# One emission order for another in a three-part kernel: first stage, last step and tail rewritten, some weight preparation on other engines

## The chip, the cores and the metric

The kernel runs on one core of one Trainium2 chip. The metric is device time in microseconds (us) of one execution; lower is better. Three executions of the kernel before gave 519.78, 521.58 and 523.94 us, a median of 521.58. The engines of a core run their own instruction queues in order: PE (TensorE, matmul), DVE (VectorE), ACT (ScalarE), POOL (GpSimd) and SP (SyncE), which here issues nearly all DMAs. They wait for each other by semaphores.

## What is computed

A gated linear attention, a two-layer network with a leaky ReLU, and a soft mixture of experts, in float32:

```python
for t in range(S):                       # attention, per batch and head; S = 768, D = 48
    state = alpha[t, :, None] * state + k[t][:, None] * v[t][None, :]
    y[t] = q[t] @ state
x = y as [3072, 384]
h = x @ w_in                             # [3072, 2048]
g = maximum(h, 0) + alpha_ff * minimum(h, 0)
x2 = g @ w_out                           # [3072, 384]
logits = x2 @ phi                        # 32 slots
slot_input = softmax(logits, over tokens).T @ x2
slot_out[e] = maximum(slot_input[e] @ w1[e], 0) @ w2[e]     # 8 experts, 4 slots each
out = softmax(logits, over slots) @ slot_out
```

## The kernel before

The 3072 tokens are cut into eight steps (i = 0 to 7) of 384 tokens, each of three chunks of 128. One step goes through these parts:

- **Preparation** (`pre_first` for step 0, `pre_gen` for the others): the decays `al` are clamped (L212), multiplied up from the left by three scans (L219, into `P`) and from the right by three more (L229, in place in `al`); then `q` is multiplied by `P` (L222, on POOL) and `k` by the result of the second scans (L234, on DVE for step 1, on POOL later). ACT checks the range of `al` in two passes (`flag`, L173).
- **Attention** (`att_chunk`), per chunk: `k` transposed on PE (L257, `kt`) and copied by ACT (L259); scores `sc` (L251), masked by DVE into `tmp` (L266); the state's increment `kv` (L277), added and scaled on DVE into the next state `S` (L285, L286), which ACT copies into a matmul layout (L290, L291); the output `y` (L297). `split_x` makes a rounded high part `xh` (ACT, L537) and the remainder `xl` (DVE, L538).
- **First layer** (`h_part`, one of 16 per step): nine logical matmuls of 128x384 with the high and low parts of x and w_in (L358), a scaled copy `tn` on ACT (L367) and a maximum on DVE (L368, `g`).
- **Second layer and logits** (`g_part`): after every fourth `g`, a matmul `lg` with the product of w_out and phi (L401). `g` is also turned for the slot sums: on PE in steps 0 and 7 (L381, `tr`), in the other steps by DVE blockwise (L386, `st`) and 32 DMAs on SP (L394, `gT`).
- **Softmax over tokens and slot sums** (`soft_gen`): logits summed by a matmul `L` (L427), exponentials, small transposes on DVE (L452), the slot sums `u` (L410 from `gT`, L416 in steps 0 and 7), accumulated by L470 or L472.
- **Weights** (`conv_gen`): w_in and w_out come as eight pairs of 768 KB of int64 bits (float64) and are turned into float32 in the kernel. The 16 pieces have letters: A, C, E, G, I, K, M, O are w_in 0 to 7; B, D, F, H, J, L, N, P are w_out 0 to 7. For each: a load (L104); the high word scaled (L111 on ACT, or L109 on DVE for the letters in `P_DVE`) and the low word scaled (L112, ACT); two integer operations on DVE (L123, L124); an addition on POOL (L125). A w_in piece is then rounded to `wi` on ACT (L128), and the remainder is taken from it (L129), on POOL for letters in `POOL_OPS`, else on DVE. A pair of w_out pieces is written to DRAM (L140), transposed on PE (L146, `wT`, three groups of four), copied by ACT into `X` (L147), and multiplied by phi (L153, `wps`).
- **Tail** (`tail_steps`): slot inputs, expert layers (L593, L614), a gather (L622, L627) and the outputs (L639, copies L642 and L644, DMAs L647). Weights w1 and w2 are loaded by `feed` (L514) and `feed_wide` (L504) in the last steps, in the order of need.

Nothing is scheduled by a tool: each part is a Python generator that emits a few instructions at a time, and four strings of letters say which generator emits next. The order of the letters is the order of the instructions on every engine's queue:

```python
    for c in START + STEADY * (NSTEP - 3) + LAST:
        next(s[c])
    k.tail()
```

`l` loads al, k, q of a step (step 0: with v, a third at a time), `w` loads v, `p` is one piece of preparation, `x`, `y`, `z` are one piece of attention of chunk 0, 1, 2, `h` one first-layer part, `g` one second-layer part, `s` one piece of softmax, `d` two small loads, `f` and `m` weight loads for the tail, `c` and `C` one step's softmax over slots (L490 to L496); capital A to P are one piece of that letter's weight preparation. START runs once, with 8 of the 128 `h`; STEADY runs five times; LAST and TAIL end the kernel.

`RAW_SLOT` names the pieces whose raw load takes a slot of its own in the pool of 22; the others share two wide buffers, two pieces to a buffer. Since a letter string sets all queues at once, moving a letter moves its DMAs on SP as well as its work on DVE, ACT, POOL and PE. A DMA waits for the eighth DMA before it and for its buffer.

Of the kernel before, what the change touches and what calls it, by code (L numbers as in the profile page):

```python
# [29 lines left out]
class Kern:  # L30
# [60 lines left out]
    def conv_gen(self, kind, n):  # L91
        nc = self.nc
        add = nc.gpsimd if CONV_NAMES[CONV.index((kind, n))] in POOL_OPS else nc.vector
        name = CONV_NAMES[CONV.index((kind, n))]
        if name in RAW_SLOT:
            raw = self.slot(f"raw{name}")
# [10 lines left out]
        yield  # L107
        if name in P_DVE:
            nc.vector.tensor_scalar_mul(out=p, in0=p, scalar1=2.0 ** -112)  # L109
# [95 lines left out]
    def pre_gen(self, i):  # L205
# [22 lines left out]
        for c, r in enumerate(parts):  # L228
# [4 lines left out]
            yield  # L233
        (nc.vector if i == 1 and "k" not in POOL_OPS else nc.gpsimd).tensor_tensor(out=k, in0=k, in1=G, op=ALU.mult)  # L234
        d["ready"] = 3
# [322 lines left out]
    def tail_steps(self):  # L558
# [72 lines left out]
        def output(ch, i):  # L631
# [13 lines left out]
            rows = self.a["out"][2 * i * T:2 * (i + 1) * T, CH * ch:CH * (ch + 1)]  # L645
            queue = nc.gpsimd if "stuvwxyz"[4 * ch + i] in TAIL[-LAST_OUT:] else nc.sync
            queue.dma_start(out=rows.rearrange("(t p) c -> p t c", p=128), in_=ot)  # L647
# [10 lines left out]
    def tail(self):  # L658
        steps = self.tail_steps()
        for c in TAIL:  # L660
            steps[c]()
# [2 lines left out]

CH = T // 2
PE_TURN = (0, NSTEP - 1)
POOL_OPS = "CDEHLNQRTVX"
LAST_OUT = 1
RAW_SLOT = "BCDEGHJLMO"
P_DVE = "KNOP"  # L670
PRE_POOL = ()
START = "lpldlpAFABxppFpxyBpCBpxyAlCxAHpyxEOFwDpMByGzwHAJCpEzCGDIppppyzzDhpEDGpphhHEIEpDxIFgxzGFDJNIJCPJBHLhGhJHxhHKLKLggyyKBhLMggMLOxKgKOlIMLPFNxyNJpNpPypppphzNzpPPPNyOpOMppg"
STEADY = "lhgzzhghghhzgxxpghghghghgpspphhxgyyspsghspxhxhgsggpghshzzywgpyypp"
LAST = "hhhhzgggghhgzghhhghggsgxxxshhghxsygyshygmxszgyzghhgghhz1zQhhfhyhggQzgghshghgfgfcghghsghfshghmQgQzhgffhcshhgghfgfggghfccfcffhfhgsghsfhgcfsgfgss2sffssfsf"
TAIL = "FabCcFFdgFCehFifkjFomFFqvlstunprzyxw"
W_ORDER = ([("w1", 4 * q + e, hf) for q in range(2) for hf in range(2) for e in range(4)]
           + [("w2", e, ch) for ch in range(2) for e in range(8)])

# [11 lines left out]
def streams(k):  # L690
    def loads():
        for c in range(3):
            k.att_load(0, ("al", "k", "q", "v"), c)
            yield
        for i in range(1, NSTEP):
            k.att_load(i, ("al", "k", "q"))
            yield

    def v_loads():
        for i in range(1, NSTEP):  # L700
            k.att_load(i, ("v",))
            yield

    def pres():
        yield from k.pre_first()
        for i in range(1, NSTEP):
            yield from k.pre_gen(i)

    def atts(c):
        for i in range(NSTEP):  # L710
            yield from k.att_chunk(i, c)

    def small():
# [33 lines left out]
def general_path(tc, nslots, ys, **a):  # L747
# [41 lines left out]
    with ExitStack() as ctx:  # L789
# [81 lines left out]
```

## Time and profile before

| | |
|---|---|
| median of three executions | 521.58 us (519.78 to 523.94) |
| profiled execution, its own time | 523.21 us |
| its span, first to last instruction | 521.1 us |
| outside the span | 2.1 us |
| mean granted TensorE clock | 0.93 of full |
| PE / DVE / ACT / POOL busy | 87% / 66% / 41% / 16% of the span |

The views are of one profiled execution. Times in them are us from the first instruction. PE's rows come in "x" counts of hardware matmuls, two to a logical one. The granted clock is a share of TensorE's full speed. A bracket at the end of a timeline row gives the idle time of the engine before it and what ended it.

### The profile page before, as it was taken

The page shows a single profiled execution, that of the slowest core. Times are in us where ns is not written, and L with a number is a line of the kernel's source. Part 1 is how long each engine was busy: PE and PEld are TensorE (multiplying, and loading weights), DVE is VectorE, ACT ScalarE, POOL GpSimd, SP SyncE. Part 2 cuts the span into 40 slices and gives each one's busy share as a digit, 9 for nine tenths or more (in the row PEclk, how much of TensorE's full clock was granted, in tenths as well). Part 3 has the DMA queues.
Part 4 walks back from the last instruction along what each step waited for, and adds up shares of the span by engine and source line. Part 5 has one row for each costly group of instructions (what it writes and reads, how often), then busy time and mean ns, then how long its engine had stood idle before and what let it go on. Part 6 is the DMA issues. An engine that isn't in the chain of part 4 may idle for free.

```text
span 521.1 us, 11082 instructions
## 1 busy us (share of the span) xinstructions
PE 454.3 (87%) x4524; PEld 371.3 (71%) x4524; DVE 345.2 (66%) x684; ACT 214.5 (41%) x408; POOL 82.2 (16%) x47
## 2 busy tenths in 40 slices
PE   2663489899999999999999999999997999959881
PEld 1452479788988887888688788788875888643561
DVE  6867963699379879869877986995673543451222
ACT  0783425763562543354244335423422345332122
POOL 1135351344002202200220220021000001000000
PEclk9985757778999999999999999999999999989986
DMA  8994440614006345645643554512664948979856
GB/s 282 406 415 188 181 182 1 232 42 178 36 2 241 79 83 115 238 100 122 243 99 69 153 207 85 122 62 59 127 182 86 332 107 313 403 306 413 355 172 199
DMA packets 41595, 93.99 MB, mean 180 GB/s; under 512 B 5056, under 2 KB 29120, under 8 KB 41536
## 3 DMA queue, kind: packets, MB, share of 16 engines
q1 hardware_dynamic: 41392, 92.61, 54.3%
q8 instruction: 37, 0.61, 0.5%
q0 software_dynamic: 144, 0.59, 0.3%
q14 instruction: 22, 0.18, 0.1%
HBM read 66.45 MB, written 7.86 MB: 143 GB/s over the span
## 4 chain that ended last, share of the span: by engine, by line
PE 70%; DVE 10%; ACT 6%; SPq 4%; DMA 4%; issue 3%; POOL 1%; ACTq 0%; POOLq 0%
PE h L358 36%; PE y L297 5%; PE lg L401 4%; PE sc L251 4%; SPq L394 4%; PE u L410 3%; PE o L614 2%; PE h L593 2%; PE wps L153 2%; PE tr L381 2%; PE kv L277 2%; DMA rawB<-w_out 2%; DVE P L219 2%; PE kt L257 2%; DVE al L229 2%
## 5 line engine op out<-in xcount | busy, mean ns | idle before, releaser
L358 PE MATMUL h<-xh,wi 128*128 128x384 f32 x768 | 221.7, 356 | 9.2 <-ACT xh L537 8.8
L358 PEld LDWEIGHTS h<-xh,wi 128*128 128x128 f32 x768 | 145.1, 194 | 28.3 <-issue 16.5
L358 PE MATMUL h<-xl,wi 128*128 128x384 f32 x384 | 132.6, 345 | 0.0
L367 ACT ACTIVATE tn<-h,alp 128x384 f32<-128x384 f32 x128 | 73.8, 583 | 128.6 <-PE h L358 123.5
L368 DVE TENSOR_TENSOR g<-h,tn 128x384 f32<-128x384 f32 x128 | 69.2, 549 | 83.7 <-ACT tn L367 75.1
L358 PEld LDWEIGHTS h<-xl,wi 128*128 128x128 f32 x384 | 74.8, 195 | 1.2 <-DVE xl L538 0.3
L386 DVE STREAM_TRANSPOSE st<-g 128x384 f32<-128x384 f32 x96 | 53.1, 564 | 0.5 <-DMA gT<-st 0.3
L222 POOL TENSOR_TENSOR q<-q,P 128x1536 f32<-128x1536 f32 x7 | 24.4, 3481 | 149.7 <-DVE Z L221 114.8
L251 PE MATMUL sc<-q,k 48*128 48x128 f32 x384 | 33.2, 313 | 2.3 <-DVE tmp L266 2.3
L297 PE MATMUL y<-tmp,v 128*32 128x128 f32 x768 | 30.4, 299 | 3.8 <-DVE xl L538 2.5
L251 PEld LDWEIGHTS sc<-q,k 48*128 48x128 f32 x384 | 27.3, 209 | 8.3 <-issue 5.0
L257 PE MATMUL kt<-cst,k 128*128 128x128 f32 x80 | 14.9, 317 | 19.7 <-DVE k L197 10.7
L266 DVE TENSOR_TENSOR tmp<-sc,cst 128x512 f32<-128x512 f32 x48 | 30.5, 675 | 1.8 <-PE sc L251 1.4
L401 PE MATMUL lg<-g,wpr 128*32 128x384 f32 x256 | 30.8, 496 | 0.8 <-DVE g L368 0.8
L297 PEld LDWEIGHTS y<-tmp,v 128*32 128x32 f32 x768 | 22.9, 119 | 9.7 <-issue 4.0
L219 DVE TENSOR_TENSOR_SCAN P<-al,Z 128x512 f32<-128x512 f32 x21 | 26.8, 1293 | 0.2
L229 DVE TENSOR_TENSOR_SCAN al<-al,Z 128x512 f32<-128x512 f32 x21 | 26.4, 1264 | 0.2
L257 PEld LDWEIGHTS kt<-cst,k 128*128 128x128 f32 x80 | 10.6, 161 | 22.0 <-DVE k L197 10.9
L234 POOL TENSOR_TENSOR k<-k,al 128x1536 f32<-128x1536 f32 x6 | 17.4, 2905 | 51.8 <-DVE al L229 51.8
L290 ACT COPY S<-S 64x256 f32<-64x256 f32 x20 | 8.1, 406 | 41.8 <-DVE S L286 37.0
L410 PE MATMUL u<-gT,dT 128*32 128x512 f32 x144 | 20.9, 596 | 1.4 <-DMA gT<-st 1.4
L490 POOL COPY cr<-c 128x384 f32<-128x384 f32 x8 | 4.0, 507 | 110.5 <-DVE st L386 57.9
(211 smaller groups left out, 594.5 us busy)
## 6 DMA issues: line engine op xcount, KB each, us to landing
w<-w SPq DMA_DIRECT2D x28, 768.0 KB, 8.6
gT<-st SPq DMA_DIRECT2D x192, 96.0 KB, 2.2
al<-alT SPq DMA_DIRECT2D x7, 768.0 KB, 5.6
k<-kT SPq DMA_DIRECT2D x7, 768.0 KB, 7.1
q<-qT SPq DMA_DIRECT2D x7, 768.0 KB, 8.5
v<-vT SPq DMA_DIRECT2D x7, 768.0 KB, 4.2
out<-ot SPq DMA_DIRECT2D x7, 576.0 KB, 4.9
w_out_f<-wo SPq DMA_DIRECT2D x4, 768.0 KB, 4.0
```

What stands on the lines that cost most here:

```text
L219: nc.vector.tensor_tensor_scan(P[:, r], al[:, r], Z[:, r], 0.0, ALU.mult, ALU.add)
L229: nc.vector.tensor_tensor_scan(G[:, r][:, ::-1], G[:, r][:, ::-1], Z[:, r][:, ::-1], 0.0, ALU.mult, ALU.add)
L251: nc.tensor.matmul(sc[h][:, p], K[r, p, c], Q[r, p, c], start=True, stop=True)
L257: nc.tensor.transpose(kt[:, p * 128:(p + 1) * 128], K[:, p, c], self.ident)
L266: nc.vector.tensor_tensor(out=m, in0=sc[h], in1=self.tri[:, None, :].to_broadcast([128, NP, 128]), op=ALU.mult)
L297: nc.tensor.matmul(y[32 * g:32 * g + 32, kt], lhsT, rhs, start=start, stop=stop, skip_group_check=True)
L358: nc.tensor.matmul(h, w[ft // 2][:, kt, fs], x[:, kt], start=(n == 0), stop=(n == 8))
L367: nc.scalar.activation(out=t, in_=h, func=AF.Copy, scale=al)
L368: nc.vector.tensor_tensor(out=g, in0=h, in1=t, op=ALU.max)
L386: nc.vector.transpose(out=self.stage.rearrange("p t b f j -> p (t b) f j")[:, :, f], in_=g.rearrange("p (n j) -> p n j", j=32))
L401: nc.tensor.matmul(self.lg[32 * jj:32 * jj + 32], self.wpr[:, 4 * fb + jj], self.g[4 * fb + jj], start=(fb == 0), stop=(fb == 3))
L410: nc.tensor.matmul(u[32 * q:32 * q + 32], dT[:, t], self.gT[q][:, t], start=(t == 0), stop=(t == 2))
```

## The change

Four tables and the letter strings differ; no function does. w_in pieces A and K take their remainders (L129) on POOL instead of DVE. The high words of C and L are now scaled on DVE (L109) and those of K and N on ACT; O and P stay on DVE. G and L give up slots of their own and N gets one, so that G shares a wide buffer with I. START has the same letters in a new order. STEADY, LAST and TAIL hold the same letters too, some of them moved by a few places.

```diff
-POOL_OPS = "CDEHLNQRTVX"
+POOL_OPS = "ACDEHKLNQRTVX"
 LAST_OUT = 1
-RAW_SLOT = "BCDEGHJLMO"
-P_DVE = "KNOP"
+RAW_SLOT = "BCDEHJMNO"
+P_DVE = "CLOP"
 PRE_POOL = ()
-START = "lpldlpAFABxppFpxyBpCBpxyAlCxAHpyxEOFwDpMByGzwHAJCpEzCGDIppppyzzDhpEDGpphhHEIEpDxIFgxzGFDJNIJCPJBHLhGhJHxhHKLKLggyyKBhLMggMLOxKgKOlIMLPFNxyNJpNpPypppphzNzpPPPNyOpOMppg"
-STEADY = "lhgzzhghghhzgxxpghghghghgpspphhxgyyspsghspxhxhgsggpghshzzywgpyypp"
...
+START = "llplpBAAFxBdppFpxpyDCpBxAClxAAypyHpFEGByCwxMzJzpHODIEpGCBPzpDpwpzhpEpGpKIhIpHJFDDEyDghxFFIhGElNJhCJJLHHxhHLGxzyLKygKBMhggLLOMKgxxKgPMLONIyppzNJNPypNhpzOPMpppPpPyNpgpO"
+STEADY = "hlzgzzhghghhpghxxpgghghghgppsxghyyspgshhspxhghgssxpghhzzypygwpypg"
...
-TAIL = "FabCcFFdgFCehFifkjFomFFqvlstunprzyxw"
+TAIL = "FFabCcFdgeFCFhifkFjoFmlFqvstunprzyxw"
```

DVE's queue, at the end of step 0's attention. Names are tile and number; `al1` and `P1` are step 1's decays and products, `St` and `S` the state after chunk 2 of step 0, `xl0` the remainder of step 0's last chunk, which the first `h` needs. Before:

```order
L212 TENSOR_SCALAR al1_241<-al1_241 128x1536
L214 COPY Z_95<-al1_241 128x12
L215 MEMSET al1_241 128x13
L219 SCALAR_TENSOR_TENSOR P1_302<-al1_241,Z_95 128x512 x3
L221 MEMSET Z_95 128x12
L285 TENSOR_TENSOR St_397<-kv_387,S_284 128x256
L286 TENSOR_TENSOR S_396<-St_397,pe_121 128x256
L538 TENSOR_TENSOR xl0_267<-y_402,xh0_266 128x3x128
```

With the change:

```order
L215 MEMSET al1_239 128x13
L285 TENSOR_TENSOR St_391<-kv_381,S_284 128x256
L286 TENSOR_TENSOR S_390<-St_391,pe_125 128x256
L219 SCALAR_TENSOR_TENSOR P1_292<-al1_239,Z_95 128x512
L123 SCALAR_TENSOR_TENSOR rawD_211<-rawD_211 128x768
L124 TENSOR_SCALAR rawD_211<-rawD_211 128x768
L219 SCALAR_TENSOR_TENSOR P1_292<-al1_239,Z_95 128x512 x2
L221 MEMSET Z_95 128x12
L538 TENSOR_TENSOR xl0_263<-y_406,xh0_262 128x3x128
```

The two state operations moved ahead of the three scans, and the two integer operations of piece D moved from behind `xl0` to between the scans.

PE's queue, between the first `h` parts (`wi0`, `wi1` are w_in 0 and 1) and step 1's first attention work (`kt` from `k1`). Before, the end of the third `h` and what follows:

```order
L358 MATMUL h_487<-xh0_266,wi1_358 128x384
L146 MATMUL wT_509<-cst_91,wo0_213 128x128 x4
L257 MATMUL kt_518<-cst_91,k1_243 128x128 x4
L251 MATMUL sc0_515<-q1_245,k1_243 128x128
L251 MATMUL sc1_516<-q1_245,k1_243 128x128
L251 MATMUL sc0_515<-q1_245,k1_243 128x128
L251 MATMUL sc1_516<-q1_245,k1_243 128x128
L381 MATMUL tr_533<-cst_91,g_446 128x128 x3
```

With the change, the end of the second `h` and what follows:

```order
L358 MATMUL h_469<-xh0_262,wi0_233 128x384
L146 MATMUL wT_495<-cst_91,wo0_216 128x128 x4
L146 MATMUL wT_501<-cst_91,wo0_216 128x128 x4
L146 MATMUL wT_509<-cst_91,wo0_216 128x128 x4
L153 MATMUL wps_515<-phi_94,X0_494 128x32 x12
L381 MATMUL tr_530<-cst_91,g_447 128x128 x3
L358 MATMUL h_535<-xh0_262,wi1_333 128x384
```

`kt` of step 1 stands right behind that third `h`. The third group of `wT`, the 12 `wps` and one `tr` moved from behind `kt` to ahead of it; before, four more `sc` stood between them.

POOL's queue, from the second weight piece to step 1's `q`. Before:

```order
L125 TENSOR_TENSOR rawA_144<-rawA_144 128x768
L125 TENSOR_TENSOR wo1_294<-rawA_144 128x768
L125 TENSOR_TENSOR rawC_211<-rawC_211 128x768
L129 TENSOR_TENSOR wi1_358<-rawC_211,wi1_358 128x768
L222 TENSOR_TENSOR q1_245<-q1_245,P1_302 128x1536
L125 TENSOR_TENSOR wo0_213<-rawD_300 128x768
```

With the change:

```order
L125 TENSOR_TENSOR rawA_144<-rawA_144 128x768
L129 TENSOR_TENSOR wi0_233<-rawA_144,wi0_233 128x768
L125 TENSOR_TENSOR wo1_294<-rawA_144 128x768
L125 TENSOR_TENSOR rawC_213<-rawC_213 128x768
L129 TENSOR_TENSOR wi1_333<-rawC_213,wi1_333 128x768
L125 TENSOR_TENSOR wo0_216<-rawD_211 128x768
L222 TENSOR_TENSOR q1_243<-q1_243,P1_292 128x1536
```

The remainder of piece A was added behind its sum, and the sum of piece D moved ahead of step 1's `q`.

Elsewhere in words. SP issues all loads of step 0 first and then B, A, F (before: A, F, B, behind two small loads). In STEADY one `h` moved ahead of `kt`, `L` stands one `h` earlier, and the `lg` that followed `u` now stands ahead of it. In LAST, groups of `ct` (L493) that stood three in a row are set apart by other matmuls. In TAIL the second and third expert outputs `o` (L614) stand together, and the first output matmuls (L639) that stood between them follow.

## Rows read from the trace of the kernel before

**Rows 1.** Page, part 1: busy us (share of span), instructions.
```profile
PE 454.3 (87%) x4524; PEld 371.3 (71%) x4524; DVE 345.2 (66%) x684; ACT 214.5 (41%) x408; POOL 82.2 (16%) x47
```

**Rows 2.** Windows: length, busy us of PE, PEld, DVE, ACT, POOL, granted clock, DMA.
```profile
39.00:52.00 13.00, 4.16 (x31) 3.35 (x23) 10.43 (x9) 5.25 (x8) 7.28 (x3) 0.50 0.47 191
52.00:65.00 13.00, 5.91 (x28) 5.49 (x26) 11.70 (x15) 5.29 (x8) 4.90 (x3) 0.76 0.49 181
65.00:78.00 13.00, 11.00 (x56) 9.80 (x56) 8.30 (x7) 2.98 (x6) 6.89 (x3) 0.50 0.49 183
117.00:130.00 13.00, 12.23 (x123) 10.96 (x123) 12.67 (x17) 4.73 (x10) 5.11 (x2) 0.87 0.46 178
...
199.00:243.00 44.00, 44.00 (x470) 36.70 (x461) 35.84 (x77) 18.49 (x39) 6.41 (x2) 1.00 0.55 148
```

**Rows 3.** Waits of PE, whole span: waiting line, releaser, us, times, longest.
```profile
PE kt L257 <- DVE k L234: 9.1, 1, 9.1
PE h L358 <- ACT xh L537: 8.8, 1, 8.8
...
PE o L639 <- DVE ss L627: 2.6, 2, 1.3
...
PE u L410 <- DMA gT<-st: 1.4, 2, 1.0
PE ct L493 <- DVE cs L496: 1.3, 1, 1.3
```

**Rows 4.** Timeline of SP and ACT: start, us, instruction, count, idle before and releaser.
```profile
16.00 0.33 SPq L104 DMA_DIRECT2D rawE<-w_in  x1
17.90 0.33 SPq L104 DMA_DIRECT2D rawO<-w_in  x1
...
16.01 0.89 ACT L111 ACTIVATE rawA<-rawA 128x768 f32<-128x768 f32 x1 [13.97 <-DMA rawA<-w_in]
16.80 0.88 ACT L112 ACTIVATE rawA<-rawA 128x768 int32<-128x768 uint32 x1
17.58 0.57 ACT L259 COPY tmp<-kt 128x512 f32<-128x512 f32 x1
18.04 0.91 ACT L111 ACTIVATE rawA<-rawA 128x768 f32<-128x768 f32 x1
```

**Rows 5.** Chain that ended last, in order of time: start, us, what.
```profile
35.73 1.56 ACT P L173 x2
...
48.94 3.53 PE h L358 x9
```

**Rows 6.** Timeline of POOL, step 1's preparation.
```profile
39.79 2.87 POOL L129 TENSOR_TENSOR wi<-rawC,wi 128x768 fp32r<-128x768 f32 x1 [2.60 <-ACT wi L128]
43.83 3.42 POOL L222 TENSOR_TENSOR q<-q,P 128x1536 f32<-128x1536 f32 x1 [1.16 <-DVE P L219]
```

**Rows 7.** Timeline of DVE, first stage.
```profile
28.92 0.96 DVE L129 TENSOR_TENSOR wi<-rawA,wi 128x768 fp32r<-128x768 f32 x1 [1.55 <-ACT wi L128]
30.25 0.43 DVE L286 TENSOR_TENSOR S<-St,pe 128x256 f32<-128x256 f32 x1
...
44.24 3.29 DVE L286 TENSOR_TENSOR S<-St,pe 128x256 f32<-128x256 f32 x1
...
53.92 1.22 DVE L229 TENSOR_TENSOR_SCAN al<-al,Z 128x512 f32<-128x512 f32 x1
55.06 0.93 DVE L123 SCALAR_TENSOR_TENSOR rawE<-rawE 128x768 int32<-128x768 int32 x1
56.03 0.56 DVE L124 TENSOR_SCALAR rawE<-rawE 128x768 int32<-128x768 int32 x1
...
65.11 1.75 DVE L234 TENSOR_TENSOR k<-k,al 128x1536 f32<-128x1536 f32 x1
```

**Rows 8.** Timeline of PE, from the wait for step 1's k.
```profile
67.00 1.09 PE L257 MATMUL kt<-cst,k 128*128 128x128 f32 x4 [9.10 <-DVE k L234]
...
71.17 1.11 PE L146 MATMUL wT<-cst,wo 128*128 128x128 f32 x4
72.08 5.36 PE L153 MATMUL wps<-phi,X 128*128 128x32 f32 x24
```

**Rows 9.** Timeline of DVE after that, a wait for ACT.
```profile
80.14 0.96 DVE L129 TENSOR_TENSOR wi<-rawI,wi 128x768 fp32r<-128x768 f32 x1 [6.65 <-ACT wi L128]
```

**Rows 10.** Timeline of PE and DVE around one turn's slot sums.
```profile
246.50 1.06 PE L410 MATMUL u<-gT,dT 128*32 128x512 f32 x6
248.58 2.31 PE L410 MATMUL u<-gT,dT 128*32 128x512 f32 x17 [1.02 <-DMA gT<-st]
...
244.57 0.52 DVE L368 TENSOR_TENSOR g<-h,tn 128x384 f32<-128x384 f32 x1
```

More of the change, by code (lines that the diff above doesn't have):

```diff
@@ L666 @@
 PE_TURN = (0, NSTEP - 1)
-POOL_OPS = "CDEHLNQRTVX"
+POOL_OPS = "ACDEHKLNQRTVX"
 LAST_OUT = 1
-RAW_SLOT = "BCDEGHJLMO"
-P_DVE = "KNOP"
+RAW_SLOT = "BCDEHJMNO"
+P_DVE = "CLOP"
 PRE_POOL = ()
-START = "lpldlpAFABxppFpxyBpCBpxyAlCxAHpyxEOFwDpMByGzwHAJCpEzCGDIppppyzzDhpEDGpphhHEIEpDxIFgxzGFDJNIJCPJBHLhGhJHxhHKLKLggyyKBhLMggMLOxKgKOlIMLPFNxyNJpNpPypppphzNzpPPPNyOpOMppg"
-STEADY = "lhgzzhghghhzgxxpghghghghgpspphhxgyyspsghspxhxhgsggpghshzzywgpyypp"
-LAST = "hhhhzgggghhgzghhhghggsgxxxshhghxsygyshygmxszgyzghhgghhz1zQhhfhyhggQzgghshghgfgfcghghsghfshghmQgQzhgffhcshhgghfgfggghfccfcffhfhgsghsfhgcfsgfgss2sffssfsf"
-TAIL = "FabCcFFdgFCehFifkjFomFFqvlstunprzyxw"
+START = "llplpBAAFxBdppFpxpyDCpBxAClxAAypyHpFEGByCwxMzJzpHODIEpGCBPzpDpwpzhpEpGpKIhIpHJFDDEyDghxFFIhGElNJhCJJLHHxhHLGxzyLKygKBMhggLLOMKgxxKgPMLONIyppzNJNPypNhpzOPMpppPpPyNpgpO"
+STEADY = "hlzgzzhghghhpghxxpgghghghgppsxghyyspgshhspxhghgssxpghhzzypygwpypg"
+LAST = "ghhhhzgggzghhhhhhgggxxgsgxshhhygsxxgyhygssgzmyzhgghghhzQz1hhfyhhfgsggzgghQghfhgghccgshghQfhzQghghfghgfshghfmsfgghcgchgfhgfffhcshgsfhgfcsggfss2sfsfssfff"
+TAIL = "FFabCcFdgeFCFhifkFjoFmlFqvstunprzyxw"
 W_ORDER = ([("w1", 4 * q + e, hf) for q in range(2) for hf in range(2) for e in range(4)]
```

## The prediction

> **What bounds the kernel now.** I read the busy shares first, then the windows, the waits of PE, and the timelines of the stretch in which PE stands still. PE is busy for 87% of the span and no other engine for more than 66% [rows 1], so the span is PE's work plus the time in which PE stands still or runs at a low clock. The windows say where that is. In a repeated turn PE is busy for 44.00 of 44.00 us at full clock: there is nothing to win there but a shorter PE queue. In the first stage it is busy for 4.16 of 13 us, then 5.91, then 11.00, at granted clocks of 0.50, 0.76 and 0.50 [rows 2]: 0.50 is the lower level, 1.2 GHz of 2.4, and it stands around the two long waits. PE's waits name these: the first `h` waits 8.8 us for `xh`, and the first `kt` of step 1 waits 9.1 us for `k` from DVE [rows 3]. Later in the first stage the bound is shared: in the window from 117 DVE is busy for 12.67 of 13.00 us and PE for 12.23 [rows 2].
>
> The change adds and removes no operation but two of placement, and has the same number of scalings on ACT and DVE. So what counts is when the two waits end, what the new order puts ahead of them, and whether DVE and POOL, which both get less room, hold something up.
>
> **The first wait: xh for the first h.** Before, this `h` starts at 48.94 [rows 5], behind a chain on DVE: the three scans of step 1, then the state operation L286, 3.29 us where the same operation took 0.43 earlier [rows 7], because POOL ran `q` from 43.83 for 3.42 us [rows 6]. The change puts the state ahead of the scans, so this chain is gone. What is late next is ACT's own queue. It starts with piece A, which now comes behind B: loads of 768 KB go out 1.90 us apart [rows 4], so ACT starts at 16.01 + 1.90 = 17.9. From there to this `xh` the new order has 17 operations on 768 columns (15 scalings, 2 casts) at 0.79 from start to start, four range checks at 1.56, and 12 small copies (3 of `kt`, 6 of the state, 3 `xh`) at 0.46 [rows 4, 5]: 13.4 + 6.2 + 5.5 = 25.1, which ends at 43.0. That is the lower bound. One pause is in sight: the state copies wait for L286, which now stands beside A's remainder on POOL. If it is blocked as before, it loses 3.29 - 0.43 = 2.9 us; I take 2. The remainder `xl` stands behind the last scans and piece D on DVE, which I count with 1 us. First `h` at 46.2, 2.7 earlier; bounds 43.0 and 48.9.
>
> **The second wait: k for kt.** Behind the first `h` PE now has a second one, three `wT`, 12 `wps`, one `tr` and a third `h` ahead of `kt`. Two ends compete.
> - PE itself: two `h` at 3.53 [rows 5] end at 53.3. `wps` needs three copies on ACT, and the rounding of piece E stands among them; that needs E's sum on POOL, which stands behind `q`. From the end of the first `h` at 49.7: its `tn` and `g` 1.1, two small operations 0.4, a scan 1.22, E's two operations 1.49 [rows 7], then sum, rounding and copy, about 2.9 by their like: 56.8, and up to 2.9 more if `q` blocks DVE. I take 59. So a new wait of some 4 us takes part of the place of the old one: PE has about 2 us of `wT` between 53.3 and 59. Then 12 `wps` 5.36 [rows 8], `tr` about 0.8, `h` 3.53: 68.7 at the lower clock, and about half of it, 64, at the upper.
> - `k`: from 50.8, when the first `g` is there: 0.4, three scans of 1.22, the two operations of E, G and I at 1.49 each, one `g` of 0.56, `k` itself 1.75 [rows 7]: 61.6. POOL's `q` and sums add 3 to 5: 64.6 to 66.6.
>
> So `kt` comes between 65 and 68.7; I take 67, the same as before. But by then PE has done what stood behind `kt` before: one `wT`, all `wps` and a `tr`, 0.9 + 5.4 + 0.8 = 7.1 us [rows 8]. The lead is 67.0 + 7.1 - 67 = 7, between 5.4 and 9. The first saving of 2.7 is inside it. The cover that makes it is work that does not need `k`; should E's rounding come late, this cover goes with it.
>
> **Does the lead last?** Only if DVE, nearly full later, gets ahead as well. Before, it stood idle for 6.65 us at 73.5 for a rounding on ACT that stood behind `wps` [rows 9]; with `wps` done earlier this wait should shrink, which is room for the 7. The two remainders that leave DVE give 2 x 0.96 = 1.9 [rows 7] and cost POOL 2 x 2.87 [rows 6]; behind A's on POOL stand F's and C's sums, for which no one waits at once, and behind K's the sum of O. If each blocks a DVE operation for its whole length, DVE loses 5.7 and gains 1.9, 3.8 net; if it hides, it gains 1.9. I take 0. The scalings are exchanged at equal counts, 0. So the first stage gives -7, bounds -9 and -2.
>
> The Trainium skill, page "SBUF — State Buffer", section "Who interferes with whom", speaks against the move: a DVE instruction with two SBUF inputs and a GpSimd instruction that reads SBUF exclude each other for a whole instruction. L286 at 3.29 beside `q` agrees [rows 6, 7]. By that rule at both places the time would be 3.8 us later than my sum, 515.4.
>
> **Turns, last step and tail.** `u` waits 1.4 us in all for `gT` [rows 3]; with `lg` ahead of it, some 0.8 us of work covers each of two waits: -1. The operands of that `lg` are there in time: its last `g` ended at 245.09 where `u` began at 246.50 [rows 10]. In LAST the `ct` in a row waited 1.3 us for DVE's `cs`, in TAIL the first output matmuls waited 1.3 for `ss` (2.6 in two waits) [rows 3]; other matmuls now stand in between. -2.6 if nothing else is late; weights for the third `o` are needed some 3 us sooner, so I take -2, bounds -2.6 and +1.
>
> **Sum.** -7 - 1 - 2 = -10. The profiled execution took 523.21 (521.1 and 2.1 outside the span), so 513.2 for it; the median of the three runs is 1.63 below it: 511.6.
>
> **Rivals.**
> - *The clock stays up.* The old wait stands in windows at 0.50, and from 65 to 78 PE worked 11.00 us at it [rows 2]. If the shorter wait leaves the clock at the upper level, half of that, 5 us, comes on top: 506.5. For it: more matmuls in a row ahead of `kt`. Against: the new wait ahead of `wps`. Chance 0.13. The page "TensorE: Matmul & The Clock Gate" of the Trainium skill, "What's actually happening", says the same in general: the low clock is the default and activity lifts it.
> - *The lead is given back on DVE and POOL.* POOL's new work blocks DVE at both places (+3.8), and some of the lead is lost in the part where DVE was busy for 12.67 of 13 us, some 3 us: 511.6 + 6.8 = 518.4. For it: DVE's share and L286. Against: the idle 6.65 us [rows 2, 7, 9]. Chance 0.20.
> - *Slower: the turns wait.* `lg` now stands ahead of `u`, so a late `g` holds both. The slack is 246.50 - 245.09 = 1.4 us [rows 10]. If in the new order DVE comes to this `g` by a scan (1.22), a state operation blocked by POOL (2.9) and a remainder (1) later [rows 7], PE waits 5.1 - 1.4 = 3.7 in each of five turns: 18.5, so 530. It decides from a delay of 3.4 us: then the five waits of 2 equal the whole gain of 10. For it: DVE is busy for 35.84 of 44 us in a turn. Against: PE at 44.00 of 44.00, so DVE has 8 us in each to catch up [rows 2]. Chance 0.10.
>
> **How the numbers follow.** Likeliest, 0.57: 511.6, own range 507 to 516. With the others the range 503 to 520 leaves out about half of the clock's case below, a few in a hundred of the second rival, and the third. A difference of 1%, 5.2 us, is about what a measurement of this kernel can tell from no change, so faster means below 516.4. Faster: nearly all of the likeliest (0.53), the clock (0.13) and a little of the second (0.02): 0.68. Within 1%: 0.04 of the likeliest, 0.17 of the second, 0.01 of the third: 0.22. Slower: 0.10 with the rest of the second and the third.
>
> **What would show it.** Right: the first `h` near 46; `kt` of step 1 near 67 with `wps` ahead of it and a wait under 2 us for `k`; a new wait of PE for `X` of about 4 us; the last scans of step 2 on DVE some 7 us earlier than before; turns of 44 us without a wait for `gT`; no 1.3 us wait at `ct` and one fewer at the outputs. Wrong: `kt` waiting over 5 us for `k`; DVE operations of 3 us beside L129 on POOL at both places and step 2's scans where they were; `lg` waiting for `g` in the turns; a wait for weights at the third `o`.

## The result and the profile after

The changed kernel takes 505.4 us in the median of four executions (502.77 to 506.15), the kernel before 521.61 (four executions). The ratio is 0.968, with a 95% interval of 0.962 to 0.973: faster by 16.2 us. That lies inside the range given (503 to 520) but below the likeliest case's own range (507 to 516): its 10 us were too few, by 6 to 7. Nearest by its number was the rival "the clock stays up", 506.5. Whether it is that rival's mechanism is what the experiments are about.

The profiled execution of after took 502.77 us, the fastest of its four, and that of before 523.21, 1.6 above its median. So the two traces differ by 20.4 us in the span, some 4 more than the medians. This spread lies in the first stage too: the kernel e11 below has the instructions of after up to the last step, and its trace reaches the first `L` at 140.20 where that of after does at 137.01. A difference of 2 or 3 us between two single traces is therefore no finding by itself, unless others repeat it.

The page's first part and the windows of after, to be laid beside [rows 1, 2]:

```profile
PE 442.8 (88%) x4524; PEld 364.2 (73%) x4524; DVE 344.2 (69%) x682; ACT 212.2 (42%) x408; POOL 84.5 (17%) x49
```

```profile
39.00:52.00 13.00, 6.51 (x29) 5.93 (x30) 9.21 (x12) 9.36 (x15) 7.55 (x3) 0.74 0.90 353
52.00:65.00 13.00, 9.31 (x45) 8.89 (x45) 12.43 (x13) 2.73 (x7) 7.82 (x4) 0.61 0.35 128
65.00:78.00 13.00, 12.26 (x107) 11.07 (x109) 9.45 (x14) 6.46 (x13) 4.46 (x3) 1.00 0.66 223
117.00:130.00 13.00, 13.00 (x95) 11.73 (x93) 3.98 (x7) 8.27 (x15) 1.13 (x1) 1.00 0.01 1
199.00:243.00 44.00, 43.74 (x453) 36.07 (x446) 36.33 (x78) 18.27 (x36) 6.42 (x2) 1.00 0.56 156
```

PE's busy time is 11.5 us less with the same 4524 instructions: less of its work ran at the lower clock (mean granted clock 0.93 before, 0.956 in after). From 65 to 78 it now works at 107 matmuls at a granted clock of 1.00, where before it worked at 56 at 0.50. In the turns PE is as good as full at 1.00, before (44.00 of 44) and after (43.74). They are a little shorter: from the first `L` to the fifth, four turns, it is 177.65 us before and 175.42 after.

The waits of PE in after (waiting line, releaser, us, times, longest), beside [rows 3]:

```profile
PE kt L257 <- DVE k L197: 10.6, 2, 8.7
PE h L358 <- ACT xh L537: 5.5, 1, 5.5
PE wps L153 <- ACT X L147: 5.5, 4, 3.7
...
PE o L639 <- DVE ss L627: 2.6, 2, 1.3
...
PE u L410 <- DMA gT<-st: 1.2, 1, 1.2
```

The wait of 9.1 us for step 1's `k` is gone (L197 is step 0's `k`, at the start of the kernel, as before), and so is that of `ct` for `cs`. The first `h` waits 5.5 instead of 8.8. A new wait of 3.7 for `X` stands ahead of the `wps`. The two waits for `ss` at the outputs are still there, both.

PE's timeline of after around the two waits (start, us, instruction, count, idle before and releaser), beside [rows 5, 8]:

```profile
43.38 0.69 PE L358 MATMUL h<-xh,wi 128*128 128x384 f32 x1 [5.52 <-ACT xh L537]
...
51.66 0.65 PE L146 MATMUL wT<-cst,wo 128*128 128x128 f32 x4 [2.11 <-ACT X L147]
52.15 0.62 PE L153 MATMUL wps<-phi,X 128*128 128x32 f32 x4
56.47 4.48 PE L153 MATMUL wps<-phi,X 128*128 128x32 f32 x20 [3.69 <-ACT X L147]
...
64.30 0.60 PE L257 MATMUL kt<-cst,k 128*128 128x128 f32 x4
```

`kt` of step 1 has no bracket: it does not wait for `k` at all, and what stood behind it before (`wT`, `wps`, `tr`) is done by then. It starts 2.7 us earlier than before, and 7.1 us of work that before was still to come is already done: a lead of 9.8.

### The profile page after: what moved, and what is told of

Same layout as the page of the kernel before. It is cut to its first block, busy times and chain, and to the rows that moved or that the text cites. A ratio compares the mean times of both kernels' runs of the same rounds, so it can differ in the third digit from the quotient of the medians.

```text
span 500.7 us, 11069 instructions
## 1 busy us (share of the span) xinstructions
PE 442.8 (88%) x4524; PEld 364.2 (73%) x4524; DVE 344.2 (69%) x682; ACT 212.2 (42%) x408; POOL 84.5 (17%) x49
## 4 chain that ended last, share of the span: by engine, by line
PE 62%; DVE 14%; ACT 7%; issue 5%; DMA 4%; POOL 3%; SPq 3%; DVEq 0%; ACTq 0%; POOLq 0%
PE h L358 33%; PE y L297 4%; PE lg L401 4%; PE u L410 3%; PE sc L251 3%; PE h L593 2%; DVE P L219 2%; PE wps L153 2%; SPq L394 2%; PE tr L381 2%; DVE g L368 2%; ACT tn L367 2%; DVE tmp L266 2%; PE u L416 2%; PE o L614 2%
## 5 line engine op out<-in xcount | busy, mean ns | idle before, releaser
L358 PEld LDWEIGHTS h<-xh,wi 128*128 128x128 f32 x768 | 142.9, 191 | 24.4 <-issue 14.2
L358 PE MATMUL h<-xl,wi 128*128 128x384 f32 x384 | 131.2, 342 | 0.0
L358 PEld LDWEIGHTS h<-xl,wi 128*128 128x128 f32 x384 | 73.6, 192 | 1.2 <-DVE xl L538 0.3
L386 DVE STREAM_TRANSPOSE st<-g 128x384 f32<-128x384 f32 x96 | 52.8, 561 | 0.3
L401 PE MATMUL lg<-g,wpr 128*32 128x384 f32 x256 | 28.4, 504 | 0.5 <-DVE g L368 0.5
L229 DVE TENSOR_TENSOR_SCAN al<-al,Z 128x512 f32<-128x512 f32 x21 | 28.3, 1355 | 0.2
L234 POOL TENSOR_TENSOR k<-k,al 128x1536 f32<-128x1536 f32 x6 | 17.5, 2909 | 49.3 <-DVE al L229 30.6
L219 DVE TENSOR_TENSOR_SCAN P<-al,Z 128x512 f32<-128x512 f32 x21 | 25.4, 1216 | 0.2
L257 PE MATMUL kt<-cst,k 128*128 128x128 f32 x80 | 13.1, 290 | 10.6 <-DVE k L197 10.6
L153 PE MATMUL wps<-phi,X 128*128 128x32 f32 x96 | 15.8, 324 | 6.3 <-ACT X L147 5.5
L153 PEld LDWEIGHTS wps<-phi,X 128*128 128x128 f32 x96 | 15.0, 244 | 7.1 <-ACT X L147 5.9
```

Source lines behind the costliest of these rows:

```text
L153: nc.tensor.matmul(ps[:, f], X[:, kt, f].rearrange("p j e -> p (j e)"), self.phi[:, kt], start=(kt == 0), stop=(kt == 2))
L219: nc.vector.tensor_tensor_scan(P[:, r], al[:, r], Z[:, r], 0.0, ALU.mult, ALU.add)
L229: nc.vector.tensor_tensor_scan(G[:, r][:, ::-1], G[:, r][:, ::-1], Z[:, r][:, ::-1], 0.0, ALU.mult, ALU.add)
L358: nc.tensor.matmul(h, w[ft // 2][:, kt, fs], x[:, kt], start=(n == 0), stop=(n == 8))
L386: nc.vector.transpose(out=self.stage.rearrange("p t b f j -> p (t b) f j")[:, :, f], in_=g.rearrange("p (n j) -> p n j", j=32))
L401: nc.tensor.matmul(self.lg[32 * jj:32 * jj + 32], self.wpr[:, 4 * fb + jj], self.g[4 * fb + jj], start=(fb == 0), stop=(fb == 3))
```

## The experiments

All times are against the kernel before, run on the same chip in the same job. The column "us" is the ratio less one, times 521.6.

| kernel | ratio (95%) | us |
|---|---|---|
| after | 0.968 (0.962 to 0.973) | -16.8 |
| e1: START and tables only | 0.980 (0.977 to 0.984) | -10.3 |
| e2: STEADY, LAST, TAIL only | 0.987 (0.982 to 0.991) | -6.9 |
| e3: after, remainders of A and K on DVE again | 0.970 (0.967 to 0.974) | -15.5 |
| e4: before, filler in the wait for `k` | 0.997 (0.994 to 1.000) | -1.8 |
| e5: after, `kt` ahead of its cover | 0.986 (0.981 to 0.991) | -7.4 |
| e6: after, filler in four waits | 0.967 (0.963 to 0.971) | -17.1 |
| e7: after, state behind the scans | 0.970 (0.965 to 0.974) | -15.8 |
| e8: before, TAIL only | 0.997 (0.994 to 1.000) | -1.5 |
| e9: before, `kt` behind its cover | 0.987 (0.983 to 0.990) | -6.9 |
| e10: e5 with filler in the wait | 0.977 (0.973 to 0.981) | -12.1 |
| e11: after, filler ahead of the last `u` | 0.963 (0.959 to 0.967) | -19.4 |
| e12: e11, `q` of step 2 later | 0.963 (0.959 to 0.966) | -19.4 |

### Which part of the change brings it: e1 and e2

e1 is after with three strings of before, e2 is before with three strings of after:

```diff
 START, POOL_OPS, RAW_SLOT, P_DVE: e1 as after, e2 as before
 STEADY, LAST, TAIL:               e1 as before, e2 as after
```

> The first stage's new order with the new tables (POOL_OPS, RAW_SLOT, P_DVE, START); STEADY, LAST and TAIL as before. By the prediction's terms the first stage alone is worth 7 us: 521.6 - 7 = 514.6. By the trace of the changed kernel, in which the last wps of step 1 ends 13.65 us and the last y of step 2 12.75 us earlier than before, it is worth 11 to 13: 509 to 511, with the granted clock at 1.00 from 65 to 91. A third theory, that the later parts give back a lead which they cannot use, has it at 516 or more.

> The kernel before with only STEADY, LAST and TAIL new. By the prediction's terms -1 for the turns and -2 for last step and tail: 518.6. By the trace of the changed kernel (the waits of u for gT 1.2 instead of 1.4, the lead growing from about 15 at the first L of the turns to 20.4 at the end) -4 to -5: 517, of which the turns have nearly nothing. If the parts add up, this and the kernel with the first stage alone give the whole 16.

Measured: -10.3 (8.4 to 12.3) and -6.9 (4.5 to 9.4). The sum, -17.2, is the change's own -16.8 within the intervals, so the parts add up. Both are larger than the prediction's terms, 7 and 3. The first stage is a little less than the 11 to 13 that the two traces show; these lie 4 us further apart than the medians.

Where the second gain lies can be read from the traces of e1 and after, which have the same START. Their last outputs are 6.6 apart: 2.5 of that between the first and the fifth `L`, 2.8 between `ut` and the last outputs, and 1.3 in the rest. The share of the turns repeats: from the first `L` to the fifth it takes 176.65 to 177.95 us in the five traces with the old STEADY and 174.94 to 175.70 in the nine with the new one, some 2 us less. 1.0 of that is the wait of `u` for `gT`; why the rest is gone, no run here shows.

### The place of kt: e5 and e9

e5 takes the cover away from after, by one letter (`x` emits `kt` of step 1 with its first scores, `D` the third `wT` and the `wps`, `g` the `tr`). e9 puts the cover alone into before (the second `x` emits the other scores); the copy of `kt` on ACT and its masks on DVE move with it:

```diff
 e5, START of after
-...FDDEyDghxFF...
+...FDDEyxDghFF...
 e9, START of before
-...EIEpDxIFgxzGFDJN...
+...EIEpDIFgzGFDxxJN...
```

> The changed kernel with kt of step 1 and its first scores moved ahead of the third wT, the wps of piece D, the tr and the third h, as they stood before; nothing else moves. The step of the prediction: this work is what covers the wait for k. In the changed kernel k ends at 61.9 and kt starts at 64.3. If the cover is what the first stage gained, TensorE now waits from 49.6 to 61.9 and does the moved work (12.6 us in the trace with its waits, 7.8 without) behind it: 4 to 7 us slower, 509.5 to 512.5. If VectorE sets the pace in any case, the work fits into later waits: 505 to 507. The prediction's 7 us of lead would be gone with it.

> The kernel before with one thing of the change done alone: kt of step 1 and its scores are moved behind the tr, the third wT and the 12 wps of piece D, on TensorE; everything else stands as before, the first h at 48.9 and k at 66.9 with it. If the place of kt is what the first stage gained, the work of 7.1 us that stood behind kt fills the wait for k: kt at 67 to 70 with a wait under 3, and 5 to 8 us faster, 513.5 to 516.5. If it takes the whole new order (E's rounding, the room on VectorE), the wps wait for X instead, and the gain is under 2: 520 or more.

PE's timeline of e5 and the window of all engines from 65, then the same two of e9, and then two rows of before to lay beside those of e9:

```profile
61.78 1.09 PE L257 MATMUL kt<-cst,k 128*128 128x128 f32 x4 [12.00 <-DVE k L234]
...
64.87 5.36 PE L153 MATMUL wps<-phi,X 128*128 128x32 f32 x24
```

```profile
65.00:78.00 13.00, 13.00 (x60) 12.86 (x59) 2.53 (x4) 4.35 (x8) 2.72 (x2) 0.60 0.38 125
```

```profile
61.97 1.06 PE L153 MATMUL wps<-phi,X 128*128 128x32 f32 x4 [3.70 <-ACT X L147]
63.61 4.47 PE L153 MATMUL wps<-phi,X 128*128 128x32 f32 x20 [0.58 <-ACT X L147]
67.90 1.09 PE L257 MATMUL kt<-cst,k 128*128 128x128 f32 x4
...
70.93 1.11 PE L146 MATMUL wT<-cst,wo 128*128 128x128 f32 x4
...
83.70 0.60 PE L257 MATMUL kt<-cst,k 128*128 128x128 f32 x4
```

```profile
65.00:78.00 13.00, 13.00 (x80) 12.18 (x80) 11.85 (x13) 5.50 (x9) 8.54 (x4) 0.62 0.52 183
```

```profile
77.25 1.09 PE L146 MATMUL wT<-cst,wo 128*128 128x128 f32 x4
...
91.42 1.06 PE L257 MATMUL kt<-cst,k 128*128 128x128 f32 x4
```

e5 is 9.4 slower than after, more than the 4 to 7 expected, and stands where e2 stands: with `kt` ahead of its cover, nearly all that the new START brings is gone, though the first `h` and `k` come as early as in after. `kt` itself starts 2.5 us earlier than in after, and waits 12.0; the work that would have filled the wait follows it at a granted clock of 0.60, 60 matmuls in the window instead of 107. DVE is busy for 2.53 us of that window: it waits for PE and does not set the pace there.

e9 brings -6.9 (5.2 to 8.8). `kt` comes at 67.90 and waits for nothing; in its place the `wps` wait 3.70 for `X`, as the prediction has it for after. The 7.1 us of `wT`, `wps` and `tr` that stand ahead of it are the gain. Most of it does not need the clock: the fourth `wT`, which follows when `kt`, scores, `tr` and `wps` are done, starts at 70.93 instead of 77.25, a lead of 6.3, and up to there `kt` takes 1.09 at the lower level in both. Behind it the clock plays a part: from 78 to 91 it is 1.00 in e9 and 0.76 before, and at `kt` of the next chunk the lead is 7.7 (83.70 against 91.42).

### The clock by itself: e4, e6 and e10

Filler is matmuls that nothing reads, put into PE's queue inside a wait. e4 has 46 of them ahead of `kt` in before, e10 64 ahead of `kt` in e5, e6 four groups in after. These matmuls, like those of `h`, stand in PE's rows once each; float32 products such as `wps` stand there twice. The function shown is that of e4; in the others it can also multiply float32 constants, for the group ahead of the last `u`.

```diff
+def fill(k):
+    w = k.wh[0]
+    t = k.ps_l.tile([128, T], F32, tag="lg", name="fill")
+    for _ in range(FILL.pop(0)):
+        k.nc.tensor.matmul(t, w[:, 0, :128], w[:, :, :128], start=True, stop=True)
...
+    s["+"] = repeat(lambda: fill(k))
 START of before, e4
-...EIEpDxIFgx...
+...EIEpD+xIFgx...
 START of e5, e10
-...FDDEyxDghFF...
+...FDDEy+xDghFF...
 START of after, e6 (D gives way once more, ahead of its wps; a fourth + stands in LAST as in e11)
-...pzhpEp...FDDEyDghx...
+...pz+hpEp...FDDEy+D+Dghx...
```

> The kernel before with 46 matmuls of 128x384 added to TensorE's queue behind the third h and ahead of kt of step 1, that is inside the wait of 9.1 us for k; they multiply the weights of piece A with themselves into the bank that lg uses later, and nothing reads the result. At 0.175 us each they fill 57.9 to 66 and delay nothing. Theory that the clock is a cause of its own: the granted clock in 65 to 91 is 1.00 instead of 0.50 and 0.76, the 15.3 us of work between kt and the fourth h's end take about half, and the kernel is 4 to 6 us faster: 516 to 518. Theory that VectorE sets the pace there: the clock is up as well, but TensorE waits for ACT and VectorE instead, and the time is 521 to 522. If activity alone does not lift the clock, nothing changes at all.

PE's timeline of e4 and the window of all engines from 65:

```profile
57.25 8.23 PE L879 MATMUL fill<-wi 128*128 128x384 f32 x46
67.33 0.63 PE L257 MATMUL kt<-cst,k 128*128 128x128 f32 x4 [1.85 <-DVE k L234]
...
85.80 1.06 PE L257 MATMUL kt<-cst,k 128*128 128x128 f32 x4
```

```profile
65.00:78.00 13.00, 10.84 (x96) 9.60 (x94) 10.66 (x10) 6.93 (x12) 6.91 (x3) 1.00 0.49 183
```

`kt` comes no earlier than before, but what follows runs at 1.00: 96 matmuls in the window instead of 56, `kt` of the next chunk at 85.80 instead of 91.42. So the lower clock behind the wait has a price of its own. Over the whole kernel it is 1.8 (0.2 to 3.3), less than the 4 to 6 expected. Why it is less stays open. The profiled pair keeps 4.7 of the 5.6 to the end, which speaks against a loss on VectorE, but its two executions lie some 2 us further apart than the medians, and where in the kernel those stand is not known.

> The kernel without the cover (kt of step 1 ahead of the third wT, the wps, the tr and the third h; 515.2 us, granted clock 0.60 in 65 to 78) with 64 matmuls of 128x384 that nothing reads in the wait of 12.0 us ahead of kt: 64 x 0.175 = 11.2, from 49.6 to 60.8. What this gets back is the part of the cover's worth that is the clock's and not the order's: the block of 15.9 us from kt at 61.8 to the end of the h's at 77.7 holds about 12 us at the lower clock, half of it 6. If the clock is about half of it: granted clock 1.00 in 65 to 78 and 509 to 511. If VectorE takes it back, as it did with most of the filler in the kernel before (1.8 at the end of 5.5 at kt of the next chunk): 513 to 515.

PE's timeline of e10 and its window from 65:

```profile
49.50 11.35 PE L884 MATMUL fill<-wi 128*128 128x384 f32 x64
62.43 0.63 PE L257 MATMUL kt<-cst,k 128*128 128x128 f32 x4 [1.59 <-DVE k L234]
...
64.13 5.32 PE L153 MATMUL wps<-phi,X 128*128 128x32 f32 x24
```

```profile
65.00:78.00 13.00, 13.00 (x62) 12.80 (x64) 3.36 (x6) 4.53 (x9) 3.27 (x2) 0.64 0.41 144
```

The time expected for half a cover came (4.7 back of 9.4), but not in that way, so it does not show that the clock is half of the cover's worth. The clock is 0.64 from 65 to 78, not 1.00: after 11.35 us of matmuls in a row and a wait of only 1.59, `kt` and `wT` run at the upper level and the `wps` at the lower, 5.32 for 24. At `kt` of the next chunk e10 leads e5 by 0.8. Most of the rest comes some 40 us later, at a place where the two kernels are the same: the lead is 0.6 at the rows below and 3.0 at the first `L`. PE's timeline and the window from 124, of e5 and then of e10:

```profile
124.59 0.88 PE L381 MATMUL tr<-cst,g 128*128 128x128 f32 x3 [3.43 <-DVE g L368]
```

```profile
124.00:128.00 4.00, 3.41 (x12) 3.44 (x13) 1.38 (x3) 0.48 (x1) 2.84 (x1) 0.50 0.00 0
```

```profile
124.02 0.52 PE L381 MATMUL tr<-cst,g 128*128 128x128 f32 x3 [3.42 <-DVE g L368]
```

```profile
124.00:128.00 4.00, 3.98 (x25) 3.96 (x26) 1.36 (x3) 1.43 (x3) 2.26 (x1) 1.00 0.02 4
```

The same wait of 3.4 us in the same order is followed by a clock of 0.50 in one and 1.00 in the other. The Trainium skill, page "TensorE: Matmul & The Clock Gate", section "What's actually happening", says that the hardware looks at the array's activity in windows that run freely and do not begin anew with the kernel; the same wait may then cost in one execution and not in the next. These two rows agree with that, and no run here shows the windows themselves.

> The changed kernel with matmuls added that nothing reads, in four waits of TensorE: 24 of 128x384 ahead of the first h, 8 ahead of the third wT, 16 ahead of the first wps, and 3 float32 ones of 128x384 ahead of the last step's u. Each is sized to end inside the wait it stands in (24 x 0.175 = 4.2 of 5.5; 1.4 of 2.1; 2.8 of 3.7; 2.6 of 2.9). Theory that the clock has a price of its own there: granted clock 1.00 in 39 to 65 instead of 0.74 and 0.61, first h 1.6 instead of 3.5, wps to third h 4.4 instead of 7.8 and the last u 2.7 instead of 5.35: 1.5 to 2.5 at the first stage, 2.5 at the end, 500.5 to 501.5 us. If VectorE takes back what the first stage wins, only the 2.5 of u: 503. If the added work delays what stands behind it: 507 or more.

e6 is the same as after within the intervals (-17.1 and -16.8). In its rows the two `h` ahead of the `wT` take 3.4 us instead of 5.1, and the `u` at the end 2.83 instead of 5.35; but the `wps` start at 56.52 as they did at 56.47, since `X` decides that, and they run at the lower level again, 4.44 for 20. `L` of the first turn comes at 139.32, later than in after's trace, but no later than in e11's (140.20), which has no filler there; so the rows show neither a gain nor a loss. By the times, e6 with all four groups (-17.1) is no better than e11 below with the fourth alone (-19.4). Filler in the first stage gained nothing that could be measured.

### The first h, and POOL: e7 and e3

```diff
 e7, START of after (the third z emits L285 and L286 of chunk 2, each p a scan)
-...CBPzpDpwpzhp...
+...CBPpDpwpzzhp...
 e3
-POOL_OPS = "ACDEHKLNQRTVX"
+POOL_OPS = "CDEHLNQRTVX"
```

> The changed kernel with the state operations L285 and L286 of step 0's second chunk put back behind the three scans of step 1 on VectorE, where they stood before; TensorE's order is the same. Theory of the prediction on the first wait: first h 4 to 5 us later, at 47.5 to 48.5, since the scans and, beside q on GpSimd, a longer L286 stand ahead of xh. What that costs at the end is open: by the prediction's sum the saving at the first h is inside the lead at kt, which is set by k and by the rounding of E, and k does not depend on the state: 505 to 506.5. If the first h starts the whole chain (h, g, the sum of E, X, wps, kt), all of it is 4 us later: 508 to 510.

> The changed kernel with the remainders of pieces A and K back on VectorE (POOL_OPS as before), all else new. If the move hides on GpSimd, as VectorE's longer operations beside it in the trace suggest (1.2 and 1.1 us lost for 2 x 0.96 saved), no change within 1 us: 504.5 to 506.5. If each L129 on GpSimd blocks a VectorE operation for its whole length (the rule that the prediction priced at 3.8 us net), this kernel is 3 to 4 us faster: 501.5 to 502.5. If the room on VectorE is what the first stage needed, it is 2 us slower: 507.5.

PE's timeline of e7:

```profile
46.21 0.69 PE L358 MATMUL h<-xh,wi 128*128 128x384 f32 x1 [8.03 <-ACT xh L537]
...
57.72 3.10 PE L153 MATMUL wps<-phi,X 128*128 128x32 f32 x20 [1.29 <-ACT X L147]
...
64.20 1.05 PE L257 MATMUL kt<-cst,k 128*128 128x128 f32 x4
```

The first `h` is 2.8 us later, less than expected, because L286 took 1.42 beside POOL and not 3.29; `kt` starts at 64.20 all the same. The time is 1.0 above that of after, which the intervals do not tell from nothing. So half of the first saving could be given back without a measurable loss, as the prediction said. But it was not quite for the reason given there: the end of PE's wait for `X` did move, by 1.25 (57.72 against 56.47), and the `wps` made it up because most of them ran at the upper level in this execution (3.10 for 20 against 4.48).

e3 is 1.3 above after, again inside the intervals: the move of the two remainders costs nothing that can be measured and brings little or nothing. The timelines of after show a cause. DVE first, then POOL, at piece A:

```profile
28.27 1.64 DVE L286 TENSOR_TENSOR S<-St,pe 128x256 f32<-128x256 f32 x1
...
27.76 1.87 POOL L129 TENSOR_TENSOR wi<-rawA,wi 128x768 fp32r<-128x768 f32 x1 [1.00 <-ACT wi L128]
```

POOL's L129 ends at 29.63 and L286 at 29.91, 0.28 later; before, `q` ended at 47.25 and the L286 beside it at 47.53, again 0.28 later [rows 6, 7]. So the DVE operation is held until POOL's ends. It lost 1.2 (1.64 against 0.43), about what was left of POOL's instruction, not a whole one. A whole one is 1.87 here; the 2.87 of [rows 6], which the prediction used, stood beside scans on DVE. At piece K a scaling on DVE of 0.55 took 1.69, 1.1 lost. 2.3 lost against 1.9 saved: near the 0 that the prediction took. The Trainium skill's page "SBUF — State Buffer", section "Who interferes with whom", has the two exclude each other until the instruction that came first is done; the ends at 29.63 and 29.91 agree, and the price is what is left of that instruction when the second one comes.

### The tail: e8

```diff
-TAIL = "FabCcFFdgFCehFifkjFomFFqvlstunprzyxw"
+TAIL = "FFabCcFdgeFCFhifkFjoFmlFqvstunprzyxw"
```

> The kernel before with only TAIL new. By the trace of the kernel with STEADY, LAST and TAIL new, the part from ut to the last output takes 37.6 us instead of 40.4: 2.8 less, 518.7. By the prediction's terms one of two waits of 1.3 for ss goes: 520.2. The rest of the 6.9 that the three parts gave together is then that of STEADY and LAST. The two waits of 1.3 for ss should both still be there, and the third o take 2.7 instead of 4.23 at a granted clock of 1.00.

The tail of before, then of after, then the last outputs of e8, on PE:

```profile
467.33 0.63 PE L568 MATMUL ut<-cst,acc 128*128 128x128 f32 x4 [0.96 <-DVE acc L472]
...
496.23 4.23 PE L614 MATMUL o<-w,ht 128*32 128x192 f32 x64
...
507.73 2.90 PE L639 MATMUL o<-ss,cs 128*128 128x192 f32 x24 [1.26 <-DVE ss L627]
```

```profile
450.46 0.63 PE L568 MATMUL ut<-cst,acc 128*128 128x128 f32 x4 [0.95 <-DVE acc L472]
...
472.84 5.41 PE L614 MATMUL o<-w,ht 128*32 128x192 f32 x128
...
480.09 2.90 PE L639 MATMUL o<-ss,cs 128*128 128x192 f32 x24 [1.32 <-DVE ss L627]
...
488.08 2.90 PE L639 MATMUL o<-ss,cs 128*128 128x192 f32 x24 [1.26 <-DVE ss L627]
```

```profile
504.89 4.52 PE L639 MATMUL o<-ss,cs 128*128 128x192 f32 x24 [1.26 <-DVE ss L627]
```

From `ut` to the last outputs it is 40.40 us before and 37.62 after: 2.8 less. Neither wait for `ss` went. What went is a third `o` at the lower clock behind such a wait (4.23; the two in a row take 5.41, 2.7 each) and short waits for `os` (0.4) and `hs` (0.2). e8 measures 1.5 (0 to 3.0), which is hardly clear of nothing and lies between the two expectations: in its trace the last outputs follow the second wait for `ss` at the lower clock, 4.52 instead of 2.90, which takes 1.6 of the 2.8.

### Beyond the change: e11 and e12

```diff
 e11, LAST of after: three float32 matmuls on constants ahead of the last u
-...sggfss2sfsfssfff
+...sggfss2sfsf+ssfff
 e12, e11 with q of step 2 on POOL behind k of step 2
-                nc.gpsimd.tensor_tensor(out=q, in0=q, in1=P, op=ALU.mult)
+                (lambda **b: i != 2 and nc.gpsimd.tensor_tensor(**b))(out=q, in0=q, in1=P, op=ALU.mult)
...
-        d["ready"] = 3
+        d["ready"] = 3 if i != 2 else (nc.gpsimd.tensor_tensor(out=q, in0=q, in1=P, op=ALU.mult), 3)[1]
```

> The changed kernel with three float32 matmuls of 128x384 that nothing reads ahead of the u of the last step, in its wait of 2.9 us for dT; nothing else. Nothing else runs beside this u that could take the time back. In the kernel with four fillers u took 2.83 instead of 5.35 and L to ut 7.6 instead of 10.1, while its first stage lost as much. Expected: 2.5 faster than the changed kernel, 502.5 to 503.5. If what the first stage lost there was no disturbance but came from this filler: 505 again.

PE's timeline of e11:

```profile
445.10 2.10 PE L886 MATMUL fill<-cst 128*128 128x384 f32 x6
448.17 2.83 PE L416 MATMUL u<-gP,dT 128*32 128x128 f32 x96 [0.97 <-DVE dT L452]
```

The three matmuls are float32 and so stand in the row as six. In after this `u` takes 5.35 at a granted clock of 0.50 behind a wait of 2.9 (4.20 before, behind the same wait). With filler in the wait it takes 2.83, and from `L` to `ut` it is 7.6 us instead of 10.1. e11's median is 503.37, 2.0 below after's; the intervals overlap, so the times alone do not prove it, but the place of the gain is in the rows, here and in e6 alike. With e12 it has the lowest median here.

> The changed kernel with the three matmuls ahead of the last u, and with one more thing: q of step 2 is multiplied on GpSimd behind k of step 2 instead of ahead of it. In every kernel with the new START the three scans L229 of step 2 run beside this q and take 6.5 us in all instead of 3.5, and where the clock is up ahead of them, TensorE waits 3.4 us for the g behind them. Theory: a cost of the new order that the prediction did not price, on the path: scans 3.5, the wait of tr for g gone or under 0.6, and 2 to 4 us less than 503.4: 499.5 to 501.5. If the q then holds up the scores of step 2 or blocks the g that now stand beside it, 503 or more.

DVE's scans of step 2, in after and in e12:

```profile
108.63 6.51 DVE L229 TENSOR_TENSOR_SCAN al<-al,Z 128x512 f32<-128x512 f32 x3
```

```profile
111.09 3.46 DVE L229 TENSOR_TENSOR_SCAN al<-al,Z 128x512 f32<-128x512 f32 x3
```

The scans lose their 3.0 us beside POOL's `q`, as expected, and the 2 to 4 us expected of it did not come: 502.95 against 503.37, the same. In e12's trace PE is busy for 11.8 and 12.5 of 13 us in the windows from 91 and 104, at a clock of 0.74 in both, and has no wait for the `g` behind the scans; e11's trace has that wait of 3.4 and a clock of 0.94 from 104 to 117. Whether the scans would count with the clock up, no run here tells.

## Why the prediction was right, and where its sizes were off

- **The first h at 46.2: it came at 43.38.** Two terms of the sum were too large. ACT began at 16.66, 0.65 later than before and not 1.9, although its first piece now loads behind another. And the pauses were 0.68 for A's sum and 0.69 for S, not 2. From 16.66 to the end of `xh` at 43.33 ACT took 26.7; the forecast's 25.1 with these pauses is 26.5. The queue was counted rightly, its start and its stops were not. The terms given, 43.0 with 2 and 1 on top, make 46.0, not 46.2. What the earlier start was worth by itself was too little to measure: e7.
- **A new wait for X of 4 us, wps at 59.** 3.69, from 52.8, with 4 of the 24 `wps` records done ahead of it; the rest go on at 56.47. The row below is ACT's: it stands idle for E's sum on POOL, as forecast, and the copy for which PE waits stands behind E's rounding.

```profile
55.03 0.90 ACT L128 CAST wi<-rawE 128x768 fp32r<-128x768 f32 x1 [2.94 <-POOL rawE L125]
55.82 0.59 ACT L147 COPY X<-wT 128x512 f32<-128x512 f32 x1
```

- **k at 64.6 to 66.6: it was done at 61.88** (L234 at 60.13, 1.75). Its chain began when the first `g` was there, at 48.1 (47.55 and 0.56) and not at 50.8, and POOL's `q` and sums added 3.4 to it, within the 3 to 5 taken.
- **kt at 67, a lead of 7: 64.30 and 9.8.** This is the term of the first stage that was mis-sized. The mechanism is the one predicted: e9 does the cover alone and gains 6.9 where the forecast has 7.1 us of covered work, 6.3 of it while PE is at the lower level behind the wait in both kernels, and e5 takes it away and loses nearly all of e1's gain. In after `kt` came out of PE's own queue, since neither end that was to hold it to 67 did.
- **The lead lasts.** It did: DVE's first `g` of the turns is at 115.20 instead of 128.34, and no wait of 6.65 on DVE is left. The rival in which DVE and POOL give it back, 518.4, was wrong in its main part, the move to POOL. DVE's busy time fell by 1.0 in all, with 1.9 of work taken from it, so its net loss by blocking is some 0.9. The largest loss that was new was not in the forecast: `q` of step 2 now blocks the scans (3.0) where before it blocked a small copy (1.94 instead of 0.16).
- **First stage -7, turns -1, last step and tail -2.** Measured -10.3 for the first and -6.9 for the rest. This is the larger miss. The turns gave some 2, by the traces, and not 1: their two waits for `gT`, 1.4 in all, are gone (one of 1.2 now stands in LAST); the rest is not explained. The `ct` no longer waits. In the tail the step "one of two `ss` waits goes" failed; in its place 1.5 came from the clock of the third `o`, 0.6 from shorter waits, and the traces show 2.8 for the tail in all. Only TAIL was run alone; the shares of STEADY and LAST are read from traces.
- **The rival of the clock.** Its sign was there: from 65 to 91 after runs at 1.00. Its 5 us on top were too many: by itself such a clock was worth 1.8 (0.2 to 3.3) in e4, and of e9's gain 6.3 us came without it. That its 506.5 lies so near the 505.4 is luck: it took 3 for the parts behind the first stage, which gave 6.9. Of the 10.3 of the new START, the cover put into before gives 6.9, and the other 3.4 has the clock from 65 on and the earlier `X` as its candidates. Taken out of after it costs 9.4, which leaves 0.9 for all the rest. So the rest counts, if at all, only with the cover in place; the difference between the two ways is hardly more than the intervals, and how it divides stays open.
- **The slower rival** did not occur: the turns have no wait of `lg` for `g` over 0.5 us.

## What to carry to other kernels

A long wait in an in-order queue is worth the independent work that can be put ahead of it: moving one instruction group past 7 us of such work gained 7 us. An earlier end of another wait further up in the same queue was worth little here, since the cover then waited for its own operands (the `wps` for `X`): half of that saving given back in e7 cost nothing that could be measured. When such a lead is summed up, add a term for what runs at a lower clock behind each wait that is left, and try filler there only where nothing else runs that the time could be lost to. Before moving a two-input operation beside one on GpSimd, look at what is left of the GpSimd instruction at that moment: that was the price at L286, twice. And read a stage from several traces before calling a difference of 2 us a result.

## What was not expected of the hardware

- Matmuls that nothing reads raise the granted clock of the work behind them like any other (0.50 to 1.00 from 65 to 78 in e4; a `u` of 5.35 to 2.83 in e11).
- They do not always: in e6 and e10 the `wps` ran at the lower level (4.44 for 20, 5.32 for 24) behind filler and a wait of 2.27 and 1.59, and in e10 other matmuls at the upper level stood between.
- The same wait of 3.4 us was followed by a clock of 0.50 in one kernel and 1.00 in another with the same order there, and their distance grew by 2.4 us up to the first `L`. In e1 the same wait was followed by the upper level (a `tr` of 0.52), in e11 by the lower (0.88). This alone is as much as some of the effects that were sought here.
